# A delta-rule attention layer and two mixing blocks on one core: the first 32-row inversion alone on VectorE in two interleaved sets, v and k in one load, shorter and later weight conversions, and other durations in the planner

## The chip, the core and the metric

One NeuronCore of a Trainium2 chip runs the whole program. The metric is device time of one execution in microseconds (us). Engines: TensorE (PE; its weight loads are PEld), VectorE (DVE), ScalarE (ACT), GpSimd (POOL) and SyncE (SP), which issues all DMAs. The granted clock of TensorE is shown as a share of 2.4 GHz: 1.00 is 2.4 GHz, 0.50 is 1.2 GHz.

## The reference, cut to what matters

```python
k_n = k / (np.linalg.norm(k, axis=-1, keepdims=True) + 1e-06)      # q, k, v: [4, 8, 768, 48]
for t in range(S):                                                  # delta rule, one state 48x48 per head
    y[:, :, t] = einsum('bhd,bhde->bhe', q[:, :, t], state)
    v_old = einsum('bhde,bhd->bhe', state, k_n[:, :, t])
    state = state + beta_t * einsum('bhd,bhe->bhde', k_n[:, :, t], v[:, :, t] - v_old)
x = y as [4, 768, 384]
h = relu(x @ w_in); u, v = halves of h                              # first mixing block, w_in 384x1024
gated = u * (w_spatial @ layernorm(v) + b_spatial); x = gated @ w_out
theta = x @ w_theta                                                 # second mixing block
u = x + w_tok_r @ (x * cos(theta)) + w_tok_i @ (x * sin(theta))
out = u + relu(u @ w_ch)
```

The weights come in as float64 (as pairs of 32-bit words); activations are float32.

## The kernel before, in words

**Attention.** The sequence is cut into chunks of 64 tokens: 12 per batch, 48 in all, each with all 8 heads side by side. In a chunk the delta rule is a linear system with a unit triangular 64x64 matrix per head. Eight chunks make a round (six rounds). `norms(r)` computes the key norms of a round; `gram(g)` makes the products of keys on TensorE (line 551), which VectorE masks and scales into `GX` (line 556; the scaled mask `gm`, line 529, is made by GpSimd, in the first round also by VectorE); `invert(r)` inverts all 32 matrices of the round at once. It copies the diagonal 32x32 blocks together (`GX<-GX`), transposes them into `un` (line 574), does 30 elimination steps of two dependent instructions each (a product, line 585, and a sum, line 590), transposes back (lines 596 and 599), and finishes the 64x64 inverse with small matmuls (`mg`, lines 615 and 621). Rounds 2 and 4 do the 60 elimination instructions on GpSimd, the others on VectorE.

`chain(g)` is serial over chunks: `ru` of the state (line 685), the right-hand side `rt` (line 689; line 678 for the first chunk of a batch), `ru` of the inverse (line 696), the copies into `W`, and the state update `s` (line 712). `py` (line 724) is the chunk's output. `jit(g)` prepares what only chunk g needs; in it v and k are loaded apart and scaled apart (lines 661 and 657).

**Mixing blocks.** All their matmuls are issued by one line, 838, in three products of split float32 (fp32r) parts; they are called big matmuls here. The first block's weights are converted from float64 (`cvt` and `vl`, 12 pieces of 256 columns) before its first big matmul. The second block's weights (`bgt` and `bgm`, 68 pieces of 192 columns) are converted beside the first block and parked in DRAM tiles until it ends. A conversion is one ScalarE instruction (the absolute value of the high word) and four on VectorE (lines 747, 752, 756 and 759).

**Order.** Nothing is issued in program order. Every piece of work is a task with durations for the engines that may do it, dependences and a priority; the class `Plan` replays engines of these durations on the host and issues the tasks in the order in which they would start. An engine takes its instructions strictly in that order. All DMAs go through SP's queue in that order, too.

## Time and profile before

| | |
|---|---|
| median of 3 runs | 847.38 us (845.59, 847.38, 847.4) |
| profiled execution, span from first to last instruction | 849.1 us |
| busy: PE, DVE, ACT, POOL | 750.6, 638.9, 330.8, 253.1 us |
| mean granted clock of TensorE | 0.906 |
| instructions on DVE, POOL | 1503, 346 |

The profile gives the profiled execution's span; no time of its own stands beside it. The span is 1.7 us above the median of the runs, so a time worked out from the span is read as a run's time with 1.7 us taken off. Busy shares are averages over stages with different limits, so the stages are read apart below.

### The profile page before, as it was taken

How to read it: one execution, taken by the hardware profiler on the slowest of the kernel's cores; microseconds unless marked ns; L12 is line 12 of the kernel's file. 1: busy time of each engine (PE TensorE's matmuls, PEld its weight loads, DVE VectorE, ACT ScalarE, POOL GpSimd, SP SyncE). 2: the span in 40 equal slices, each digit the busy share in tenths (PEclk: the TensorE clock that was granted, in tenths of full speed). 3: DMA queues.
4: the chain of work that ended last, by engine and by line, in shares of the span. 5: the costliest groups of instructions: out<-in, count | busy, mean ns of one | idle time of the engine just before them, and what ended most of it. 6: DMA issues, size and time to landing. Idle time of an engine off the chain costs nothing. (4 is left out here: it accounts for less than half of the span.)

```text
span 849.1 us, 21902 instructions
## 1 busy us (share of the span) xinstructions
PE 750.6 (88%) x8672; PEld 689.2 (81%) x8672; DVE 638.9 (75%) x1503; ACT 330.8 (39%) x747; POOL 253.1 (30%) x346
## 2 busy tenths in 40 slices
PE   4317799899898897999998999979999999999998
PEld 4216677678886786888777999969999999999997
DVE  6899998997989779599876666387575565658544
ACT  4326237434244543243654334145332332333331
POOL 2442633476523358633221010032211111111010
PEclk8555589888899889999998999989999999999999
DMA  8826356676367666645666570234011101001001
GB/s 237 231 64 164 93 166 170 166 196 170 89 171 211 175 173 189 192 120 167 187 180 165 161 225 1 74 119 137 26 44 63 26 25 56 25 25 63 19 2 56
DMA packets 101701, 102.42 MB, mean 121 GB/s; under 512 B 10848, under 2 KB 86624, under 8 KB 101600
## 3 DMA queue, kind: packets, MB, share of 16 engines
q1 hardware_dynamic: 101600, 101.03, 41.5%
q8 instruction: 68, 1.11, 0.6%
q14 instruction: 33, 0.27, 0.1%
HBM read 74.38 MB, written 22.41 MB: 114 GB/s over the span
## 5 line engine op out<-in xcount | busy, mean ns | idle before, releaser
L838 PE MATMUL m<-w,vh 128*128 128x256 f32 x576 | 116.0, 301 | 1.0 <-ACT uT L364 1.0
L838 PEld LDWEIGHTS m<-w,vh 128*128 128x128 f32 x576 | 93.8, 201 | 4.5 <-ACT uT L364 1.2
L838 PE MATMUL y<-wr,z 128*128 128x384 f32 x432 | 87.9, 341 | 0.0
L838 PE MATMUL y<-w,z 128*128 128x384 f32 x432 | 85.0, 340 | 0.0
L838 PE MATMUL m<-w,vl 128*128 128x256 f32 x288 | 83.8, 291 | 0.0
L838 PEld LDWEIGHTS y<-wr,z 128*128 128x128 f32 x432 | 77.0, 190 | 0.0
L838 PEld LDWEIGHTS y<-w,z 128*128 128x128 f32 x432 | 75.5, 188 | 0.0
L838 PEld LDWEIGHTS m<-w,vl 128*128 128x128 f32 x288 | 57.6, 200 | 0.0
L696 PEld LDWEIGHTS ru<-rt,GX 64*64 64x64 f32 x384 | 30.4, 155 | 25.2 <-DVE rt L689 17.9
L696 PE MATMUL ru<-rt,GX 64*64 64x48 f32 x384 | 36.7, 243 | 15.7 <-DVE rt L689 14.4
L657 POOL TENSOR_TENSOR kc<-kc,gam 128x192 f32<-128x192 f32 x36 | 22.4, 623 | 93.1 <-DMA kc<-in_kn_dram 73.9
L838 PE MATMUL m<-wo,gh 128*128 128x384 f32 x192 | 48.8, 335 | 1.1 <-DVE rr L1145 1.1
L364 ACT ACTIVATE W<-ru 64x192 f32<-64x192 f32 x88 | 28.6, 326 | 53.8 <-PE ru L697 52.0
L615 PE MATMUL mg<-xt,GX 32*32 32x32 f32 x768 | 18.8, 203 | 34.6 <-DVE xt L596 27.8
L1143 DVE TENSOR_SCALAR ni<-m 128x384 int32<-128x384 f32 x24 | 13.3, 555 | 47.8 <-PE m L838 47.8
L529 POOL TENSOR_TENSOR gm<-mask,gam 128x256 f32<-128x256 f32 x59 | 39.5, 671 | 29.3 <-DVE pp L560 10.8
L615 PEld LDWEIGHTS mg<-xt,GX 32*32 32x32 f32 x768 | 16.0, 118 | 38.8 <-DVE xt L596 28.9
L585 DVE TENSOR_TENSOR tmp<-un 128x30 f32<-128x30 f32 (+14 forms) x120 | 46.4, 387 | 1.2
L838 PE MATMUL m<-xTh,wih 128*128 128x256 f32 x144 | 47.1, 327 | 0.0
L590 DVE TENSOR_TENSOR un<-un,tmp 128x30 f32<-128x30 f32 (+14 forms) x120 | 45.9, 383 | 1.2
L770 POOL TENSOR_TENSOR gl<-graw,gh 128x512 fp32r<-128x512 f32 x11 | 14.8, 1342 | 96.7 <-DVE gh L370 80.3
L364 ACT ACTIVATE bgm<-bgr 128x192 f32<-128x192 f32 x68 | 25.3, 375 | 45.2 <-DMA wdr<-bgm 12.1
(191 smaller groups left out, 2285.2 us busy)
## 6 DMA issues: line engine op xcount, KB each, us to landing
kq<-in_kqT_dram SPq DMA_DIRECT2D x96, 128.0 KB, 3.6
kg<-in_kqT_dram SPq DMA_DIRECT2D x32, 256.0 KB, 3.2
gd<-gt SPq DMA_DIRECT2D x24, 256.0 KB, 2.8
graw<-gd SPq DMA_DIRECT2D x24, 256.0 KB, 2.8
k<-in_kn_dram SPq DMA_DIRECT2D x24, 192.0 KB, 3.8
v<-in_vn_dram SPq DMA_DIRECT2D x48, 96.0 KB, 2.5
kc<-in_kn_dram SPq DMA_DIRECT2D x48, 96.0 KB, 3.1
xd<-xs SPq DMA_DIRECT2D x48, 96.0 KB, 2.7
```

The costliest lines, as they stand in the source:

```text
L364: nc.scalar.activation(out=out, in_=in_, func=func, **kw)
L529: eng[e].tensor_tensor(out=gm.t, in0=mask.t.unsqueeze(1).to_broadcast([128, HP, CH]), in1=gam[r].t[:, j].unsqueeze(2).to_broadcast([128, H ...
L585: eng[e].tensor_tensor(out=t3, in0=un.t[:, k:k + 1, 0:k].to_broadcast([128, m, k]), in1=un.t[:, k + 1:32, k:k + 1].to_broadcast([128, m, k ...
L590: eng[e].tensor_tensor(out=un.t[:, k + 1:32, 0:k], in0=un.t[:, k + 1:32, 0:k], in1=t3, op=ALU.add)
L615: mm(out=ps.t[q + 32:q + 64, u, :], lhsT=gx[q:q + 32, u0 + u, 32:64], rhs=xt.t[q:q + 32, u0 + u, :], start=True, stop=True, tile_position= ...
L657: lambda e: eng[e].tensor_tensor(out=kc.t, in0=kc.t, in1=gam[r].t[:, j].unsqueeze(2).to_broadcast([128, HP, D]), op=ALU.mult),
L696: mm(out=pu.t[64:128, hp, :], lhsT=gx[64:128, u, :], rhs=rt.t[64:128, hp, :], start=True, stop=True)
L770: P.add(o_tts(n), lambda e: eng[e].tensor_tensor(out=lv(), in0=mv(), in1=hv().bitcast(F32), op=ALU.subtract), [m, h], [(l, part)], pr)
L838: mm(out=view(), lhsT=a, rhs=c, start=(start and q == 0 and s_ == 0), stop=(stop and q == tot - 1 and s_ == 2))
L1143: P.add(o_dve(DM), lambda e: nc.vector.tensor_scalar(out=ni.t, in0=th(), scalar1=1.0 / TWO_PI, scalar2=None, op0=ALU.mult), [ps], [ni], pr)
```

## The change

1. **The first inversion.** In round 0 each elimination step is split over the even and the odd columns (`sets`), each with a scratch tile of its own: product even, product odd, sum even, sum odd. It makes 118 instructions of half the size out of 60. A list `inv0` holds the task that ends this inversion (the transpose back into `GX`); other VectorE work waits for it by `after=inv0`: the norms' reduction and the masks of later rounds, the first block's weight conversions and splits, the products in `jit`. The other rounds keep their 60 instructions.
2. **Loads.** v and k of a chunk lie beside each other in DRAM and come in one DMA of 192 KB into `vk`; one instruction of 384 columns scales both (for the first three chunks ScalarE does it in 24 small instructions). The norms read k by fours, not by twos. `G1P` puts the Gram products of round 1 at a later priority.
3. **Conversions.** The scratch `t` is gone. The absolute value is raised to a smallest number, masked and shifted in place: two instructions with one input and two with two inputs, where one with one input and three with two inputs stood. The second block's pieces are 384 columns wide (34 instead of 68 of each instruction), and they may start only when chunk 16's `ru` of the inverse has been issued (`BG0`).
4. **The planner.** Its durations are replaced (for instance a group of 8 matmuls 490 ns for 648), and it now models the time a semaphore takes from each engine to each other, a lock between VectorE and GpSimd for work that is not from PSUM, bytes and landings of DMAs, and a change of matmul kind on PE. So the order changes everywhere.

```diff
-KN = 4
+KN = 2
+KB = 4
-G1P = -19.8
-BGW = 192
+G1P = -9.5
+BGW = 384
+BG0 = 16
+ACTV = 3
...
-    SAME = {"PE": 0.0, "ACT": 60.0, "DVE": 127.0, "POOL": 90.0, "SP": 0.0, "X": 0.0}
-    CROSS = 190.0
+    SAME = {"PE": 0.0, "ACT": 142.0, "DVE": 126.0, "POOL": 133.0, "SP": 0.0, "X": 0.0}
+    TAIL = {"PE": 185.0, "ACT": 112.0, "DVE": 90.0, "POOL": 55.0, "SP": 0.0, "X": 0.0}
+    LAT = {"PE": 54.0, "ACT": 35.0, "DVE": 35.0, "POOL": 78.0, "SP": 27.0, "X": 0.0}
...
+                    if e == "SP":
+                        s = max(s, lands[-LANES])
+                    if e in self.HELD and held[e] != t.part:
+                        s = max(s, free[e] + self.HELD[e])
+                    if t.port and e in lock:
+                        b0, b1 = lock["POOL" if e == "DVE" else "DVE"]
+                        if b0 <= s < b1:
+                            s = b1
...
-        v_b[g] = r_v.new()
-        load(v_b[g], lambda: v_b[g].t, vn[b, c], 98304, pr)
-        kc_b[g] = r_kc.new()
-        load(kc_b[g], lambda: kc_b[g].t, kn[b, c], 98304, pr)
+        vk = vk_b[g] = r_vk.new()
+        load(vk, lambda: vk.t, vkn[b, c], 196608, pr)
...
+        sets = [(0, 1)] if not cr else [(0, 2), (1, 2)]
+        ub = [Buf(tile_=un.t) for _ in sets]
+        fin = [[] for _ in sets]
+        heads = []
         for k in range(30, 0, -1):
-            m = 31 - k
-            tmp = r_tmp.new()
...
+            for half in (0, 1):
+                for i, (c0, st) in enumerate(sets):
+                    t0 = k + 1 + (k + 1 - c0) % st
+                    m = len(range(t0, 32, st))
+                    if m <= 0:
+                        continue
+                    if half == 0:
+                        tmp = fin[i] = r_tmp.new()
...
+                                                 in1=un.t[:, t0:32:st, k:k + 1].to_broadcast([128, m, k]), op=ALU.mult)
...
+                            eng[e].tensor_tensor(out=un.t[:, t0:32:st, 0:k], in0=un.t[:, t0:32:st, 0:k], in1=t3, op=ALU.add)
...
+        if cr:
+            inv0.append(P.tasks[-1])
...
+        vk = vk_b[g]
+        if g < ACTV:
+            for i in range(2):
+                def fv(e, i=i):
+                    for hp in range(HP):
+                        act(vk.t[:, i, hp], vk.t[:, i, hp], ACTF.Copy, scale=ng_b[r].t[:, j, i, hp:hp + 1])
+
+                A([("ACT", 4 * 235.0)], fv, [ng_b[r]], [vk], pr)
+            return
+        A([("DVE", d_dve(384)), ("POOL", 880.0)],
+          lambda e: eng[e].tensor_tensor(out=vk.t, in0=vk.t, in1=ng_b[r].t[:, j].unsqueeze(3).to_broadcast([128, 2, HP, D]),
+                                         op=ALU.mult), [ng_b[r]], [vk], pr, after=inv0)
...
+        P.add([("DVE", d_dve2(n))], lambda e: nc.vector.tensor_scalar(
+            out=m.t, in0=m.t, scalar1=TINY_LO, scalar2=None, op0=ALU.max), [], [m], pr, after=inv0)
+        P.add([("DVE", d_dve2(n))], lambda e: nc.vector.tensor_scalar(
+            out=mi(), in0=mi(), scalar1=0x07FFFFFF, scalar2=3, op0=ALU.bitwise_and, op1=ALU.logical_shift_left), [], [m], pr)
+        P.add(o_dve(n), lambda e: nc.vector.scalar_tensor_tensor(
+            out=mi(), in0=lo(), scalar=29, in1=mi(), op0=ALU.logical_shift_right, op1=ALU.bitwise_or), [raw], [m], pr)
+        P.add(o_dve(n), lambda e: nc.vector.scalar_tensor_tensor(
+            out=mi(), in0=hi(), scalar=-0x40000000, in1=mi(), op0=ALU.bitwise_and, op1=ALU.bitwise_or), [raw], [m], pr)
```

What the new plan does to the order shows at two places on VectorE. The first is the beginning of round 0's inversion. `GX_108` is round 0's matrix and `GX_109` round 1's; `gm` is a scaled mask, `cvt` the scratch of a weight conversion, `un` and `tmp` belong to the inversion. Before:

```order
L513 SCALAR_TENSOR_TENSOR gam<-gam,beta_sb 128x32
L747 TENSOR_SCALAR cvt<-vh 128x256
L529 TENSOR_TENSOR gm<-mask,gam 128x256
L556 TENSOR_TENSOR GX_109<-gp,gm 128x256 x2
L529 TENSOR_TENSOR gm<-mask,gam 128x256
L574 STREAM_TRANSPOSE un<-GX_108 128x1024
L575 MEMSET un 128x32
L556 TENSOR_TENSOR GX_109<-gp,gm 128x256
L585 TENSOR_TENSOR tmp<-un 128x30
L590 TENSOR_TENSOR un<-un,tmp 128x30
L585 TENSOR_TENSOR tmp<-un 128x58
L556 TENSOR_TENSOR GX_109<-gp,gm 128x256
```

And now:

```order
L592 TENSOR_TENSOR GX_108<-gp,gm 128x256 x3
L407 COPY GX_108<-GX_108 32x32x32
L611 STREAM_TRANSPOSE un<-GX_108 128x1024
L612 MEMSET un 128x32
L633 TENSOR_TENSOR tmp<-un 128x30
L633 TENSOR_TENSOR tmp<-un 128x29
L641 TENSOR_TENSOR un<-un,tmp 128x30
L633 TENSOR_TENSOR tmp<-un 128x29
L641 TENSOR_TENSOR un<-un,tmp 128x29 x2
```

The work on round 1's norms and matrix and on the weights no longer stands ahead of or between the elimination steps. The six `GX_109` products that stood between them, and the two ahead of them, come behind the inversion.

The second place is the end of the same inversion, with the first chunk's right-hand side `rt`. Before, these rows led up to it, behind the transposes back and one copy; `ss` and `k` belong to later norms, `vl`, `vh` and `wil_138` to the weights:

```order
L747 TENSOR_SCALAR cvt<-vh 128x256
L499 TENSOR_REDUCE ss<-k 128x8
L770 TENSOR_TENSOR wil_138<-vl,wih_135 128x256
L752 SCALAR_TENSOR_TENSOR cvt<-vh,cvt 128x256
L499 TENSOR_REDUCE ss<-k 128x8
L756 SCALAR_TENSOR_TENSOR cvt<-vh,cvt 128x256
L759 SCALAR_TENSOR_TENSOR vl<-vl,cvt 128x256
L503 TENSOR_SCALAR ss<-ss 128x32
L678 TENSOR_SCALAR rt<-v 128x192
```

And now:

```order
L641 TENSOR_TENSOR un<-un,tmp 128x15 x2
L734 TENSOR_SCALAR rt<-vk 128x192
L646 STREAM_TRANSPOSE xt_620<-un 128x32x32
L649 STREAM_TRANSPOSE GX_108<-un 128x32x32
L407 COPY GX_108<-GX_108 32x32x32
L802 TENSOR_SCALAR vl<-vl 128x256 x2
L804 TENSOR_SCALAR vl<-vl 128x256 x2
L806 SCALAR_TENSOR_TENSOR vl<-vh,vl 128x256 x2
L808 SCALAR_TENSOR_TENSOR vl<-vh,vl 128x256 x2
```

The right-hand side now stands straight behind the last elimination step; the conversions of the first block's weights, two pieces of which stood ahead of `rt` before, all stand behind the inversion.

## Rows read from the trace of the kernel before

**Rows 1.** Stretches: us, then busy us (instructions) by engine; PEclk, DMA share, GB/s.

```profile
21.00:58.00 37.00, 8.53 (x142) 7.08 (x140) 33.19 (x71) 10.54 (x21) 13.09 (x18) 0.50 0.56 159
66.00:138.85 72.85, 59.38 (x1062) 50.00 (x1062) 71.50 (x196) 35.40 (x92) 32.27 (x39) 0.69 0.50 140
138.85:234.95 96.10, 85.44 (x1235) 74.01 (x1228) 85.04 (x201) 37.91 (x89) 57.11 (x94) 0.86 0.58 162
234.95:372.10 137.15, 123.33 (x2096) 105.64 (x2090) 112.80 (x289) 57.81 (x142) 66.13 (x106) 0.93 0.64 176
372.10:482.00 109.90, 103.23 (x1707) 88.09 (x1700) 84.09 (x245) 53.11 (x136) 23.80 (x30) 0.95 0.61 171
482.00:849.10 367.10, 358.04 (x2206) 352.36 (x2202) 230.14 (x445) 122.50 (x249) 49.75 (x41) 0.99 0.19 60
```

**Rows 2.** Stretches, line 696 alone (8 instructions a chunk): PE, PEld, PEclk, DMA.

```profile
66.00:138.85 72.85, 7.38 (x64) 6.24 (x64) 0.69 0.50 140
138.85:234.95 96.10, 6.56 (x64) 5.46 (x64) 0.86 0.58 162
234.95:372.10 137.15, 11.35 (x128) 9.33 (x128) 0.93 0.64 176
```

**Rows 3.** Timeline ahead of the first inversion: start, us, instruction, [idle before, releaser].

```profile
15.20 0.74 DVE L556 TENSOR_TENSOR GX<-gp,gm 128x256 f32<-128x256 f32 x2
16.46 0.42 DVE L556 TENSOR_TENSOR GX<-gp,gm 128x256 f32<-128x256 f32 x1 [0.52 <-PE gp L551]
18.42 0.43 ACT L364 ACTIVATE vl<-vh 128x256 f32<-128x256 f32 x1 [2.82 <-DMA vh<-in_w_in_dram]
18.86 2.12 ACT L364 ACTIVATE GX<-GX 32x1024 f32<-32x1024 f32 x2
21.02 1.95 DVE L574 STREAM_TRANSPOSE un<-GX 128x1024 f32<-128x1024 f32 x1 [0.57 <-ACT GX L364]
```

**Rows 4.** Timeline of VectorE and GpSimd in the first inversion.

```profile
23.34 0.18 DVE L585 TENSOR_TENSOR tmp<-un 128x30 f32<-128x30 f32 x1
...
43.98 1.07 DVE L590 TENSOR_TENSOR un<-un,tmp 128x228 f32<-128x228 f32 x1
45.08 0.39 DVE L585 TENSOR_TENSOR tmp<-un 128x220 f32<-128x220 f32 x1
...
53.86 0.21 DVE L590 TENSOR_TENSOR un<-un,tmp 128x30 f32<-128x30 f32 x1
...
42.69 2.10 POOL L770 TENSOR_TENSOR w<-gt,w 128x384 fp32r<-128x384 f32 x2 [1.89 <-ACT w L364]
```

**Rows 5.** Timeline of VectorE behind the first inversion.

```profile
57.89 0.68 DVE L370 COPY GX<-GX 32x1024 f32<-32x1024 f32 x1
...
65.70 0.25 DVE L678 TENSOR_SCALAR rt<-v 128x192 f32<-128x192 f32 x1
```

**Rows 6.** Groups by line and form on VectorE: count, busy us, mean ns, idle before.

```profile
L752 DVE SCALAR_TENSOR_TENSOR bgt<-bgr,bgt 128x192 int32<-128x192 int32 x68 | 29.9, 440 | 1.0
L756 DVE SCALAR_TENSOR_TENSOR bgt<-bgr,bgt 128x192 int32<-128x192 int32 x68 | 29.4, 432 | 1.1
L759 DVE SCALAR_TENSOR_TENSOR bgm<-bgm,bgt 128x192 f32<-128x192 f32 x68 | 27.7, 407 | 4.2 <-ACT bgm L364 2.4
L747 DVE TENSOR_SCALAR bgt<-bgr 128x192 int32<-128x192 int32 x68 | 23.6, 347 | 9.2 <-DMA bgr<-in_w_i_dram 3.9 <-DMA bgr<-in_w_r_dram 1.9 <-DMA bgr<-in_w_out_dram 1.2
L1147 DVE SCALAR_TENSOR_TENSOR rr<-ni,rr 128x384 f32<-128x384 int32 x24 | 14.4, 598 | 0.7
L1150 DVE TENSOR_SCALAR rr<-rr 128x384 f32<-128x384 f32 x24 | 8.6, 357 | 0.7
```

**Rows 7.** Timeline of GpSimd: first and last step of round 2's inversion.

```profile
166.68 0.23 POOL L585 TENSOR_TENSOR tmp<-un 128x30 f32<-128x30 f32 x1 [1.00 <-DVE un L574]
...
222.57 0.26 POOL L590 TENSOR_TENSOR un<-un,tmp 128x30 f32<-128x30 f32 x1
```

**Rows 8.** The chain that ended last: start, us, what.

```profile
511.21 31.55 PE m L838 x231
```

More of the change, by code (lines that the diff above doesn't have):

```diff
@@ L109, with add @@
 class Task:
-    __slots__ = ("opts", "fn", "deps", "prio", "extra", "crit", "users", "left", "eng", "start", "end", "allocs", "uid", "big", "act", "credit", "order", "banks")
+    __slots__ = ("opts", "fn", "deps", "prio", "extra", "crit", "users", "left", "eng", "start", "end", "allocs", "uid", "big", "act", "credit", "order", "banks", "port", "part", "mode")
 class Plan:
     ENGS = ("PE", "ACT", "DVE", "POOL", "SP", "X")
-    SAME = {"PE": 0.0, "ACT": 60.0, "DVE": 127.0, "POOL": 90.0, "SP": 0.0, "X": 0.0}
-    CROSS = 190.0
+    SAME = {"PE": 0.0, "ACT": 142.0, "DVE": 126.0, "POOL": 133.0, "SP": 0.0, "X": 0.0}
+    TAIL = {"PE": 185.0, "ACT": 112.0, "DVE": 90.0, "POOL": 55.0, "SP": 0.0, "X": 0.0}
+    LAT = {"PE": 54.0, "ACT": 35.0, "DVE": 35.0, "POOL": 78.0, "SP": 27.0, "X": 0.0}
+    HELD = {"ACT": 138.0, "DVE": 107.0}
     def __init__(self):
         self.tasks = []
-    def add(self, opts, fn, reads=(), writes=(), prio=0.0, extra=0.0, crit=False, after=(), big=False, act=0.292):
+    def add(self, opts, fn, reads=(), writes=(), prio=0.0, extra=0.0, crit=False, after=(), big=False, act=0.292,
+            port=True, part=0, mode=1):
         t = Task()
+        t.port, t.part, t.mode = port, part, 0 if big else mode
         t.big, t.act, t.credit = big, 0.98 if big else act, 0.0
@@ L226, in run @@
         free = dict.fromkeys(self.ENGS, 0.0)
+        held = dict.fromkeys(self.ENGS, 0)
+        lock = {"DVE": (0.0, 0.0), "POOL": (0.0, 0.0)}
+        mode = 0
+        lands, dmaq = [0.0] * LANES, 0.0
         cand = [t for t in self.tasks if t.left == 0]
@@ L243, in run @@
                     for d in deps:
-                        x = d.end + d.extra + (self.SAME[e] if d.eng == e else self.CROSS)
+                        x = d.end + d.extra + (self.SAME[e] if d.eng == e else self.TAIL[d.eng] + self.LAT[e])
                         if x > r:
@@ L271, in run @@
             if e == "PE":
-                if t.big and not self.pbig:
-                    t.start = s = s + 67.0
-                self.pbig = t.big
+                if t.mode != mode:
+                    t.start = s = s + (100.0 if mode else 140.0)
+                mode = t.mode
                 t.end = self.pe_run(t, s, dur)[0]
@@ L278, in run @@
                     self.credit -= dur
+            if e == "SP":
+                dmaq = max(dmaq, t.end + DMA_PRE) + dur.n / DMA_BW
+                t.extra = dmaq + DMA_POST - t.end
+                lands.append(dmaq + DMA_POST)
             free[e] = t.end
+            held[e] = t.part
+            if t.port and e in lock:
+                lock[e] = (s, t.end - (45.0 if e == "POOL" else 0.0))
             for b in t.banks:
@@ L529, in f @@
             eng[e].tensor_tensor(out=gm.t, in0=mask.t.unsqueeze(1).to_broadcast([128, HP, CH]),
-                                 in1=gam[r].t[:, j].unsqueeze(2).to_broadcast([128, HP, CH]), op=ALU.mult)
-        A([("POOL", 575.0)] + (o_dve(256) if pr < -10 else []), f, [gam[r], mask], [gm], pr, crit=pr < -10).order.add(mt)
+                                 in1=ng_b[r].t[:, j, 1].unsqueeze(2).to_broadcast([128, HP, CH]), op=ALU.mult)
+        A([("POOL", 575.0)] + (o_dve(256) if pr < -10 else []), f, [ng_b[r], mask], [gm], pr, crit=pr < -10, after=inv0).order.add(mt)
         return gm
@@ L601, in invert @@
+        A([("DVE", 1900.0)], lambda e: nc.vector.transpose(out=gx[:, :, 0:32].rearrange("p u t -> p t u"), in_=un.t),
+          [un] + ub, gg, pr + 0.1, crit=cr, port=False)
+        if cr:
+            inv0.append(P.tasks[-1])
         for q in (1, 3):
             A(o_cps(1024), lambda e, q=q: copy(e, gx[32 * q:32 * q + 32, :, 32:64], gx[32 * q:32 * q + 32, :, 0:32]),
-              [], [gg[q]], pr + 0.2, crit=cr)
+              [], [gg[q]], pr + 0.2, crit=cr, part=32 * q)
         for q in (1, 3):
@@ L648, in jit @@
                                                                             in1=gm.t[p0:p0 + 64], op=ALU.mult),
-                  [ps, gm], [(kq, True)], pr)
+                  [ps, gm], [(kq, True)], pr, port=False, part=p0, after=inv0)
         else:
@@ L770, in split @@
         P.add(o_tts(n), lambda e: eng[e].tensor_tensor(out=lv(), in0=mv(), in1=hv().bitcast(F32), op=ALU.subtract),
-              [m, h], [(l, part)], pr)
+              [m, h], [(l, part)], pr, after=inv0)
     r_wsp = ring("w3", "w3", [128, S], F32R, 2 * NT)
```

237 lines of the change are left out of this document (109 added, 128 removed).

## The prediction

> **What bounds the kernel now.** I read the busy times by stretch first, then the starts of the chunks, then the timeline where the first stretch is lost.
>
> From 482 us to the end TensorE is busy 358.0 of 367.1 us at a clock of 0.99 [rows 1]: all chunks are done, and only big matmuls are left. Nothing in the change touches their number, so this tail can only lose what has been done earlier. It bounds the end: whatever brings the last chunk forward brings the end forward.
>
> The chain of chunks runs from 66 to 482 us. Line 696 has 8 instructions a chunk, so the counts say where chunks begin [rows 2]: chunk 8 at 138.85 us, chunk 16 at 234.95, chunk 32 at 372.1. In the stretch to chunk 8 VectorE is busy 71.5 of 72.85 us: it is the bound there, and every microsecond added or taken counts. To chunk 16 it is busy 85.0 of 96.1 us, but there GpSimd inverts round 2, from 166.7 to 222.8 us [rows 7], and chunk 16 needs that; its 0.23 and 0.26 us first and last steps stand 56 us apart. From chunk 16 to 32 TensorE (123.3 of 137.15 us) and VectorE (112.8) are both nearly full, and from 372 us TensorE is (103.2 of 109.9) while VectorE has 26 us to spare [rows 1].
>
> Before 66 us there is no chain. In the 37 us from 21 to 58 us TensorE does 8.5 us of work and VectorE 33.2 [rows 1]: the first inversion is on VectorE and nothing else can go on. This is where the change acts first.
>
> **The start.** Round 0's last `GX` ends at 16.88 us; ScalarE's copies follow only at 18.86 us, because ahead of them stands a weight's `vl` that waits for its DMA until 18.42, and the transpose starts at 21.02 [rows 3]. Now one copy goes to VectorE (0.68 us, the row of [rows 5]) beside ScalarE's single one (half of 2.12 us), and the weights' loads stand ahead of eight other loads. The norms wait for a larger load now, which I put at 0.8 us. I take the transpose at 18.0 us, 3 us earlier; bounds 17.5 and 20.5.
>
> The 60 steps run from 23.34 to 54.07 us, 30.7 us [rows 4]. A step starts 0.03 us after the one before ends (43.98 + 1.07 to 45.08), so one of 30 elements, which lasts 0.21 us, costs 0.24 and one of 220 elements 0.42: about 0.2 us and 1/960 us an element. The smallest of the first steps are a little quicker (0.18), so I use 0.19 + n/960. Both halves of all steps have 9,920 elements, 10.3 us; 60 x 0.19 + 10.3 = 21.7 us clean. The other 9 us are round 1's six products between the steps and steps that take 1.07 us where their neighbour takes 0.39, under a GpSimd product from SBUF (42.69 to 44.79) [rows 4]. `inv0` keeps both away.
>
> The 118 half steps: each needs the result of two steps back, not of the last one. Two products of 256 elements without a dependence take 0.74 us together, where one takes 0.42 [rows 3]: a second one costs 0.32, or 0.055 + n/960. The planner's order puts an independent instruction between any dependent pair, and I take 0.066 us a step (some pairs are small): 118 x 0.066 + 10.3 = 18.1 us. If nothing overlaps, it is 118 x 0.19 + 10.3 = 32.7 us. The row for independent products is the nearest, so I take 18.1.
>
> The skill speaks against this edit: the Trainium skill, VectorE: DVE Perf Modes, section The DRAIN you can't avoid, says that the next VectorE instruction waits for the pipe of the last one to empty, with or without a semaphore, and its rules for authors ask for fewer instructions. The pair of 0.74 us disagrees, but it reads PSUM. By that rule the steps take the 32.7 us of the paragraph above and the start gains 14.6 us less, and this is a rival below.
>
> So the steps end at 18.0 + 2.1 + 0.2 + 18.1 = 38.4 us, where before it was 54.07. From the last step to chunk 0's line 696 it was 12.0 us: 4.5 us until the copy's end at 58.57, and then 7.1 us in which `rt` stood behind conversions and reductions until 65.70 [rows 5]. `rt` is now ahead of the transposes. Left are the transposes (3.8), the longer of the two copies (1.06), and, as I put them, 2 us of GpSimd's clearing, for which the matrices now wait, and 1.6 us of `mg` and its copy: about 8.5 us. Chunk 0 at 47 us instead of 66: **-19 us** (bounds: -4.5 without overlap, -21).
>
> **What comes back behind it.** Work on round 1 that stood ahead of the inversion or in it is done after it now: the 4.1 us that VectorE had from 16.88 to 21.02 [rows 3], six `GX_109` products at 0.42, and four reductions of 384 elements, which at the 0.42 us of 256 are 2.5 us: about 9 us. Two weight conversions more come to 3.3 us at the price below. VectorE has no room there (71.5 of 72.85 us). Against it stand the three pieces of second-block weights that were done before chunk 8 and now start behind chunk 16: a piece of 192 columns costs 0.440 + 0.432 + 0.407 + 0.347 = 1.63 us [rows 6], 4.9 us together. 9 + 3.3 - 4.9 is **+7 us** (bounds 12 if the second-block pieces were done in gaps, 4 if steps of 1 us fall away as above); chunk 8 at about 127 us.
>
> **The conversions.** 384 columns cost 2 x 1.63 = 3.25 us. The new form has two instructions with one input, for which the nearest row is 0.357 us at 384 columns, and two with two inputs, 0.598 [rows 6]: 1.91 us. That is 1.34 us less for each of 34, 46 us of VectorE in all. But it is worth something only where VectorE is waited for. By the order of instructions, 13 old pieces (21 us) stood before chunk 16's right-hand side, and none does now; 28 (46 us) stood between chunks 16 and 32, and now 15 of the new (29 us). To chunk 16 the inversion on GpSimd sets the pace: it begins once round 2's Gram products are done, near chunk 11, and those come sooner with a freer VectorE; it shares GpSimd with 11 other instructions instead of 14. I take **-5 us** of the 21 (bounds 0 and -12). Between chunks 16 and 32 the relief is 17 us, but the order also has 408 big matmuls there where 330 were: 78 at 31.55/231 = 0.137 us [rows 8] are 10.7 us of a TensorE with 14 us to spare. I take **0** (bounds -12 and +10). From 32 on VectorE had room; **0** (bounds 5 either way).
>
> **v and k together.** 48 loads fewer, and one instruction of 384 columns for two of 192. At a chunk every 9 us and three buffers, the scaling is needed two chunks after the load: its cover is 18 us against under 2 us of landing and scaling more. Without that cover it would cost up to 1 us a chunk. The first three chunks' 24 small ScalarE instructions lie beside the 18 us of steps, with ScalarE busy 10.5 of 37 us there [rows 1]; priced at the 0.43 us of 256 columns [rows 3] or less, they take at most 10 us. Both cost nothing.
>
> **The tail.** In the order 990 big matmuls stood before chunk 47's line 696, now 1,074. These 84 no longer lie behind it: 84 x 0.137 = 11.5 us, less as they are mostly of the shorter kind; **-10 us**. The rest of the tail is as full as before and unchanged.
>
> **Sum.** -19 + 7 - 5 + 0 + 0 - 10 = -27: a span of 849.1 - 27 = 822.1 us, and with the 1.7 us by which the span stands above the median **820 us**.
>
> **Rivals.**
> - *The half steps don't overlap.* 14.6 us of the start go: 820 + 14.6 = 835 us. For it: the steps of the trace all wait for their predecessor, so no row shows an overlap of two from SBUF alone. Against: the pair of 0.74.
> - *TensorE binds the chain.* It was busy 371 of 416 us; with 84 big matmuls more and the full debt, the start is given back: -19 + 12 + 0 + 10 - 10 = -7, 840 us. For it: the 123.3 of 137.15. Against: at 0.69 and 0.86 of the clock up to chunk 16 a busy TensorE is not a full one.
> - *The clock falls (slower).* The granted clock from 66 to 482 us averages 0.88, at 1.2 GHz in parts. If the new order of small and big matmuls leaves it lower, the busy 371 us stretch in proportion: the 27 us are lost at 0.82, and at 0.80 they are +37, 857 us. For it: nothing but the sensitivity; the first big matmuls come between chunks 3 and 4 in both orders. Against: the order has as many big matmuls ahead of each chunk or more.
> - *VectorE's relief counts in full.* -19 + 4 - 12 - 12 - 2 - 10 = -51, 796 us, if GpSimd's inversions start as early as VectorE lets them.
>
> **Chances.** Forecast (806 to 831) 0.58; no overlap 0.12; TensorE binds 0.13; the clock 0.08; full relief 0.09. Within 0.3% of 847.4 (2.5 us, about what a measurement of this kernel can tell from no change) fall parts of the second and third rivals: 0.03. Slower is the rest of the clock's: 0.08. Faster 0.89. The range is 800 to 845 us: it leaves out the clock and half of the full relief, 0.13.
>
> **What would show it.** Chunk 0's line 696 near 47 us, chunk 8 near 127, chunk 16 near 215, the last chunk near 465. The steps of round 0 from about 20 to 38 us, with starts 0.07 us + n/960 apart; if they lie 0.19 + n/960 apart, the first rival is right. No step of 1 us there. VectorE's busy time down by some 50 us. It is wrong if chunk 8 comes no earlier than 135 us, if chunk 16 waits for GpSimd as late as before, or if the stretch from 66 us shows a clock well under 0.88.

## The result and the profile after

The changed kernel takes 822.0 us (median of 4 runs, 819.97 to 824.94), the kernel before 846.49 us beside it; the ratio is 0.972 (95% interval 0.9687 to 0.9753). The forecast was 820 us in a range of 800 to 845. The profiled execution has a span of 821.2 us. The total came out within 2 us, but two of its terms were wrong by 12 and 6 us, in opposite directions, so much of that agreement is luck.

Busy times of the page; TensorE and VectorE have 13.9 and 40.2 us less than before:

```profile
PE 736.7 (90%) x8672; PEld 677.4 (82%) x8672; DVE 598.7 (73%) x1377; ACT 341.2 (42%) x757; POOL 222.8 (27%) x299
```

The stretches between the same chunks as in [rows 1] (the clock's records begin at 67.8 us in this execution, and what lies before is counted as 1.00: the 1.00 of the first row is no granted clock, and the 0.79 of the second is too high; from 67.8 us to chunk 8 it is 0.72, where before it was 0.69):

```profile
17.00:38.00 21.00, 3.12 (x32) 2.42 (x32) 20.89 (x122) 8.08 (x30) 0.00 (x0) 1.00 0.64 193
45.50:137.30 91.80, 68.33 (x1196) 58.66 (x1192) 83.95 (x222) 44.03 (x99) 40.12 (x48) 0.79 0.49 142
137.30:222.60 85.30, 81.31 (x1254) 72.01 (x1252) 52.92 (x112) 29.83 (x67) 51.95 (x87) 0.93 0.42 118
222.60:355.30 132.70, 125.47 (x2178) 107.28 (x2170) 117.82 (x269) 66.62 (x153) 62.55 (x92) 1.00 0.74 215
355.30:461.20 105.90, 98.87 (x1684) 84.06 (x1680) 86.27 (x209) 53.74 (x131) 19.05 (x18) 0.98 0.70 202
461.20:821.20 360.00, 348.58 (x2127) 342.99 (x2126) 219.72 (x417) 128.37 (x262) 39.65 (x36) 0.99 0.18 58
```

The `ru` of the inverse (line 752 now, 8 instructions a chunk; the 65th of the first row is chunk 8's first), as in [rows 2]:

```profile
45.40:137.30 91.90, 7.41 (x65) 6.27 (x65) 0.79 0.49 142
137.30:222.60 85.30, 5.67 (x64) 4.65 (x64) 0.93 0.42 118
222.60:355.20 132.60, 10.58 (x128) 8.60 (x128) 1.00 0.74 215
```

Chunk 0 begins at 45.5 us (66.1 before), chunk 8 at 137.3 (138.9), chunk 16 at 222.6 (235.0), chunk 32 at 355.3 (372.2), chunk 47 at 461.2 (481.7). So 20.6 us are won at chunk 0, 1.6 are left at chunk 8, and 27.9 are there at the end.

VectorE's timeline at the first inversion, against [rows 3] to [rows 5], and at the transposing of round 1:

```profile
15.46 0.68 DVE L407 COPY GX<-GX 32x1024 f32<-32x1024 f32 x1
16.55 1.95 DVE L611 STREAM_TRANSPOSE un<-GX 128x1024 f32<-128x1024 f32 x1 [0.40 <-ACT GX L401]
18.57 0.15 DVE L633 TENSOR_TENSOR tmp<-un 128x30 f32<-128x30 f32 x1
...
30.21 0.48 DVE L633 TENSOR_TENSOR tmp<-un 128x108 f32<-128x108 f32 x2
30.58 0.48 DVE L641 TENSOR_TENSOR un<-un,tmp 128x108 f32<-128x108 f32 x2
30.96 0.48 DVE L633 TENSOR_TENSOR tmp<-un 128x110 f32<-128x110 f32 x2
...
37.39 0.25 DVE L734 TENSOR_SCALAR rt<-vk 128x192 f32<-128x192 f32 x1
...
78.06 1.93 DVE L611 STREAM_TRANSPOSE un<-GX 128x1024 f32<-128x1024 f32 x1
```

The 118 half steps take 18.9 us where the 60 took 30.7. Four of 108 elements start in 0.75 us, 0.19 us apart, though a pair of them lasts 0.48. None takes 1 us, and GpSimd does nothing beside them (0.00 in the first row of the stretches).

What VectorE does from the end of this inversion to the transposing of round 1, 42 to 78 us (the six costliest groups: count, busy us, mean ns, idle before):

```profile
L534 DVE TENSOR_REDUCE ss<-k 128x16 f32<-128x768 f32 x6 | 5.5, 945 | 1.2 <-ACT k L401 1.1
L802 DVE TENSOR_SCALAR vl<-vl 128x256 f32<-128x256 f32 x10 | 4.8, 495 | 0.0
L806 DVE SCALAR_TENSOR_TENSOR vl<-vh,vl 128x256 int32<-128x256 int32 x8 | 4.5, 566 | 0.0
L815 DVE TENSOR_TENSOR wil<-vl,wih 128x256 fp32r<-128x256 f32 x7 | 4.0, 571 | 0.0
L804 DVE TENSOR_SCALAR vl<-vl 128x256 int32<-128x256 int32 x9 | 3.8, 429 | 0.0
L808 DVE SCALAR_TENSOR_TENSOR vl<-vh,vl 128x256 int32<-128x256 int32 x8 | 3.3, 428 | 0.0
```

The five rows of first-block weights (all but the first) add up to 20.4 us of these 36, or to 17.8 when each instruction is counted only until the next one starts; 8 of the 12 pieces are finished before round 1 is transposed, where before the change there were 3. Round 1's transposing now comes 4.2 us later than before (it was at 73.82 us).

GpSimd's inversion of round 2, first and last step, against [rows 7]: 45.3 us instead of 56.1.

```profile
164.22 0.24 POOL L633 TENSOR_TENSOR tmp<-un 128x30 f32<-128x30 f32 x1
...
209.21 0.27 POOL L641 TENSOR_TENSOR un<-un,tmp 128x30 f32<-128x30 f32 x1
```

Its 60 steps take 32.8 us of these (33.4 before); 11 other instructions stand between them (14), 7.1 us (9.8); and GpSimd is idle 6.1 us there instead of 13.8 (neighbours overlap a little, so the three add up to a bit more than the whole).

The second block's conversions, against [rows 6]:

```profile
L808 DVE SCALAR_TENSOR_TENSOR bgm<-bgr,bgm 128x384 int32<-128x384 int32 x34 | 21.1, 620 | 0.3
L806 DVE SCALAR_TENSOR_TENSOR bgm<-bgr,bgm 128x384 int32<-128x384 int32 x34 | 20.6, 608 | 0.3
L802 DVE TENSOR_SCALAR bgm<-bgm 128x384 f32<-128x384 f32 x34 | 16.0, 474 | 9.3 <-ACT bgm L401 9.2
L804 DVE TENSOR_SCALAR bgm<-bgm 128x384 int32<-128x384 int32 x34 | 14.5, 430 | 0.3
```

A piece costs 2.13 us in the mean (1.82 by the median durations 359, 355, 554 and 555 ns; some are stretched to 1 us and more), 1.12 less than 3.25. By medians it is 0.84 less: two of the old half-size pieces are 2.66 us (259, 358, 357 and 358 ns an instruction).

One sum that the prediction did not make: a span is TensorE's busy time and its idle time. Before, these were 750.6 and 98.5 us; now 736.7 and 84.5. Half of the gain is TensorE waiting less, half is the same 8672 matmuls taking less time. From 67.8 us on, where both executions have a record, TensorE's clock is at 0.50 for 62.5 us; before, it was for 111.1.

### The profile page after: what moved, and what is told of

Read it like the earlier page. It is cut to its first block, busy times and chain, and to the rows that moved or that the text cites. A ratio compares the mean times of both kernels' runs of the same rounds, so it can differ in the third digit from the quotient of the medians.

```text
span 821.2 us, 21423 instructions
## 1 busy us (share of the span) xinstructions
PE 736.7 (90%) x8672; PEld 677.4 (82%) x8672; DVE 598.7 (73%) x1377; ACT 341.2 (42%) x757; POOL 222.8 (27%) x299
## 4 chain that ended last, share of the span: by engine, by line
PE 56%; DVE 26%; DMA 8%; issue 4%; ACT 2%; SPq 2%; POOL 2%; POOLq 0%; DVEq 0%; ACTq 0%
PE m L882 27%; PE y L882 19%; DVE tmp L633 4%; DVE un L641 4%; DMA vk<-in_vkn_dram 2%; PE gp L587 2%; DMA kq<-pp 2%; PE ru L752 1%; PE py L780 1%; DMA bgr<-in_w_r_dram 1%; DVE GX L649 1%; PE s L768 1%; DVE xt L646 1%; PE ru L741 1%; DMA k<-in_vkn_dram 1%
## 5 line engine op out<-in xcount | busy, mean ns | idle before, releaser
L882 PE MATMUL m<-w,vh 128*128 128x256 f32 x576 | 110.8, 291 | 1.7 <-DVE gt L990 1.2
L882 PEld LDWEIGHTS m<-w,vh 128*128 128x128 f32 x576 | 88.9, 190 | 5.4 <-DVE gt L990 1.3
L565 POOL TENSOR_TENSOR gm<-mask,ng 128x256 f32<-128x256 f32 x63 | 41.8, 670 | 75.8 <-DVE pp L596 52.3
L1188 DVE TENSOR_SCALAR ni<-m 128x384 int32<-128x384 f32 x24 | 13.3, 556 | 57.8 <-PE m L882 57.8
L633 DVE TENSOR_TENSOR tmp<-un 128x58 f32<-128x58 f32 (+23 forms) x149 | 49.1, 348 | 0.9
L752 PEld LDWEIGHTS ru<-rt,GX 64*64 64x64 f32 x384 | 28.3, 145 | 24.5 <-DVE rt L745 19.7
L641 DVE TENSOR_TENSOR un<-un,tmp 128x58 f32<-128x58 f32 (+23 forms) x149 | 44.5, 316 | 0.7
L401 ACT ACTIVATE x<-m 128x384 f32<-128x384 f32 x15 | 7.3, 489 | 87.0 <-PE m L882 87.0
L882 PE MATMUL m<-xTl,wih 128*128 128x256 f32 x144 | 41.0, 285 | 0.0
L882 PE MATMUL m<-xTh,wil 128*128 128x256 f32 x144 | 40.9, 284 | 0.0
L587 PE MATMUL gp<-kg 48*64 48x128 f32 x512 | 37.9, 289 | 3.1 <-DVE pp L596 1.8
L882 PE MATMUL m<-wt,xh 128*128 128x384 f32 x144 | 37.4, 341 | 2.8 <-ACT xh L401 2.8
```

The lines of the kernel that those rows point to most:

```text
L401: nc.scalar.activation(out=out, in_=in_, func=func, **kw)
L565: eng[e].tensor_tensor(out=gm.t, in0=mask.t.unsqueeze(1).to_broadcast([128, HP, CH]), in1=ng_b[r].t[:, j, 1].unsqueeze(2).to_broadcast([12 ...
L587: mm(out=pv()[o:o + 64, hp, :], lhsT=kh, rhs=kg.t[i:i + D, :, hp, :] if fused else kh, start=True, stop=True)
L633: eng[e].tensor_tensor(out=t3, in0=un.t[:, k:k + 1, 0:k].to_broadcast([128, m, k]), in1=un.t[:, t0:32:st, k:k + 1].to_broadcast([128, m, k ...
L641: eng[e].tensor_tensor(out=un.t[:, t0:32:st, 0:k], in0=un.t[:, t0:32:st, 0:k], in1=t3, op=ALU.add)
L752: mm(out=pu.t[64:128, hp, :], lhsT=gx[64:128, u, :], rhs=rt.t[64:128, hp, :], start=True, stop=True)
```

## The experiments

All are edits of the changed kernel. Most edits lead the planner to a new order of everything; where the order was kept, the text says so. Differences are against 822.0 us, and the ratio is to the kernel before on the same chip. The kernel before took 843.4, 844.6 and 843.6 us beside these runs and 846.5 beside the changed kernel, which did not run again with them; so a difference of 3 us or less is not to be read, and small ones are given by the ratios, too.

**Dependent half steps.** One task issues a set's product and sum together:

```diff
-                        heads.append(A([(en, dur)], fa, ...))
...
-                        A([(en, dur)], fb, ...).order.update(heads[-3:])
+                A([(en, 4 * d_dve((31 - k) * k / 2))], fp, [], [un] + tms, ...)   # fp: product, sum of even; product, sum of odd
```

> The 118 half steps of round 0 stay, but in the order product even, sum even, product odd, sum odd, so that about 74 of them need the result of the step just ahead (59 sums, and every second product of an even set) and 44 do not. Everything else that VectorE does stands behind them as in the changed kernel. Theory A (the steps of the changed kernel overlap because neighbours are independent): dependent steps cost 0.19 us + n/960, independent ones 0.066 us + n/960, so the inversion's steps take 74 x 0.19 + 44 x 0.066 + 10.3 = 27.3 us where the changed kernel took 18.9. Theory B (a half step is cheap whatever stands ahead of it): 19 us. Theory C (no two steps ever overlap, and something else made the 18.9): 118 x 0.19 + 10.3 = 32.7 us. The second question is what the first inversion's time is worth at the end: if all VectorE work up to chunk 8 is queued behind it (theory P, it passes through), chunk 0, the transposing of round 1 and chunk 8 all come some 8 us later and the kernel takes 828 us (825 to 831). If it is given back on the way (theory Q), chunk 0 comes 8 us later, chunk 8 less than 3 us later, and the kernel takes 822 to 824 us.

845.24 us (1.0011, 0.9979 to 1.0044). The steps took 26.1 us (18.6 to 44.7): theory A. Chunk 0 came 7.1 us later and chunk 8 5.5, but chunk 32 17.6, and behind the last chunk 2,118 big matmuls were left instead of 2,022. Further on the new order was another one, so the 23 us do not answer the second question. The next run does: the product is issued straight ahead of its sum, and the planner isn't told.

```diff
-                        heads.append(A([(en, dur)], fa, ...))
+                        late[i] = fa
+                        heads.append(A([(en, dur)], lambda e: None, ...))
...
+                            late[i](e)      # in fb: the product is issued straight ahead of its sum
```

> The same dependent order of the half steps as in e1_dependent_steps (each product straight ahead of its sum), but the planner isn't told: every other instruction of every engine stands where it stands in the changed kernel. So the first 7 us or so of e1_dependent_steps come without its new order from chunk 8 on. Theory P (a microsecond in VectorE's queue ahead of chunk 8 is a microsecond at the end, as 7.4 us at chunk 8 were 10.1 at the end without the first weights): steps of 26 us, chunk 0 near 52.6, chunk 8 at 143 to 145, 828 to 831 us. Theory R (the queues, made for earlier times, lose much more behind it): 835 us or more. Theory Q (it is given back by chunk 16 or later): 821 to 824 us.

827.48 us (0.9821, 0.9769 to 0.9872): half a microsecond below theory P's range, 5.5 us more than the changed kernel (8.5 by the ratios). Its VectorE timeline:

```profile
34.11 0.26 DVE L633 TENSOR_TENSOR tmp<-un 128x108 f32<-128x108 f32 x1
34.41 0.27 DVE L645 TENSOR_TENSOR un<-un,tmp 128x108 f32<-128x108 f32 x1
34.60 0.28 DVE L633 TENSOR_TENSOR tmp<-un 128x120 f32<-128x120 f32 x1
34.91 0.28 DVE L645 TENSOR_TENSOR un<-un,tmp 128x120 f32<-128x120 f32 x1
```

A sum starts 0.30 us after the product that it needs; the next product, which does not need that sum, starts 0.19 us after it. The first is 0.19 + 108/960, the second close to 0.066 + 108/960 = 0.18: both of the prediction's prices, in one row of instructions. Five of the six executions took 826.0 to 831.5 us, and the profiled one, the only one with a trace, 838.1; in it TensorE ran at half its clock for 24 us while it was fully busy:

```profile
417.10:440.90 23.80, 23.80 (x333) 21.53 (x334) 12.73 (x36) 11.04 (x27) 2.02 (x2) 0.50 0.47 138
```

**No hold.** `inv0` stays empty:

```diff
-        if cr:
-            inv0.append(P.tasks[-1])
```

> The list inv0 stays empty: no VectorE work is held back until round 0's inversion ends; everything else is as changed, in a new plan. Theory P (only the sequence of a full VectorE changes): the steps stretch from 18.9 us to 26 to 32 us and chunk 0 comes at 52 to 58 us instead of 45.5, but the work on round 1 and on the first weights is done earlier by as much, so round 1's transposing stays within 3 us of the changed kernel's 78.1 us, chunk 8 within 4 us of 137.3 us and the whole within 820 to 826 us. Theory H (keeping the inversion alone is where the gain is, since work between the steps also breaks their pairs and brings GpSimd's products beside them): chunk 8 at 143 us or later and 830 us or more.

825.86 us (0.9811, 0.9778 to 0.9844), 3.9 us more than the changed kernel (7.7 by the ratios). The total is theory P's; the way is neither's. The steps took 21.3 us, chunk 0 came at 54.7 us, round 1's transposing at 89.9 (not within 3 us of 78.1) and chunk 8 at 146.1, but chunk 16 at 209.7, 13 us earlier than in the changed kernel.

**First weights left out.** VectorE's four instructions of each first-block piece are not issued; the order is kept:

```diff
+        skip = n < 384
-        P.add([("DVE", d_dve2(n))], lambda e: nc.vector.tensor_scalar(
+        P.add([("DVE", d_dve2(n))], lambda e: None if skip else nc.vector.tensor_scalar(      # and the three behind it
```

> VectorE leaves out the four instructions of each of the 12 conversions of the first block's weights (48 instructions, 16.8 us at 0.28, 0.28, 0.41 and 0.41 us, more where they were stretched); the planner believes that they are there, so the order of everything else is that of the changed kernel. The weights of the first block are then not converted. Theory D (the loss behind the start is VectorE's work: round 1's transposing and its 43 us of steps stand in one queue with the conversions, and chunk 8 waits for that inversion): round 1's transposing comes at 66 to 72 us instead of 78.1, its last step at 106 to 114 instead of 124.2, chunk 8 at 121 to 128 us instead of 137.3; the kernel ends 4 to 12 us earlier, 810 to 818 us, since GpSimd's inversion of round 2 and TensorE take over later. Theory E (chunk 8 is held by TensorE at half its clock, or by the chain of chunks itself): chunk 8 moves by less than 4 us and the whole by less than 2 us.

812.93 us (0.9648, 0.9617 to 0.9679): theory D, with less than its numbers ahead of chunk 8. Round 1's transposing:

```profile
71.09 1.95 DVE L611 STREAM_TRANSPOSE un<-GX 128x1024 f32<-128x1024 f32 x1 [0.29 <-ACT GX L401]
```

7.0 us earlier; the last step at 116.4 us, chunk 8 at 129.9 (7.4 earlier), chunk 16 7.9, chunk 32 8.9, chunk 47 9.8, the end 10.1 earlier (9.1 by the medians of the runs, 6.1 by the ratios). VectorE's busy time fell by 14.6 us in all, so not every microsecond taken out of its queue comes through: from 41.4 us to this transposing VectorE is idle for 7.5 us, where it was for 2.9 in the changed kernel. What does come through to the transposing is there at chunk 8 and, roughly, at the end.

**Chain first.** The first four chunks get priority:

```diff
-        pr = float(g)
+        pr = g - 30.0 if g < 4 else float(g)
```

> The tasks of the chain of chunks 0 to 3 get priorities ahead of round 1's and the weights' work (g - 30 for g), so that the right-hand sides of chunks 1, 2 and 3 no longer stand behind them in VectorE's queue; in the order 11 rows of chunk 1's way and some 40 of chunk 2's go behind. Theory D (chunk 8 waits for round 1's inversion, and chunks 1 to 7 have time): chunk 2 comes at 64 to 72 us instead of 80.5, but round 1's transposing stays at 77 to 81 us, chunk 8 at 134 to 140 us, and the whole at 819 to 825 us. Theory F (the loss is the place of the right-hand sides of chunks 1 and 2, which come 5 and 11 us after their operands are there): chunk 8 comes 8 to 12 us earlier, near 127 us, and the whole 5 to 10 us, 812 to 817 us.

839.15 us (0.9952, 0.9922 to 0.9982), outside both. VectorE's rows of chunks 1 to 3 and round 1:

```profile
54.70 0.36 DVE L745 TENSOR_TENSOR rt<-ru,vk 128x192 f32<-128x192 f32 x1
62.58 0.36 DVE L745 TENSOR_TENSOR rt<-ru,vk 128x192 f32<-128x192 f32 x1 [0.79 <-PE ru L742]
69.42 0.35 DVE L745 TENSOR_TENSOR rt<-ru,vk 128x192 f32<-128x192 f32 x1
82.42 2.01 DVE L611 STREAM_TRANSPOSE un<-GX 128x1024 f32<-128x1024 f32 x1
```

Chunk 2 came 17 us earlier, at 63.5 us. Round 1's transposing came 4.4 us later, and chunk 8 7.6 us later, at 144.9. So theory F is refuted, as far as an order of its own can show it: it is not the place of the right-hand sides that holds chunk 8.

**The old price of the conversions**, the order kept:

```diff
-            out=m.t, in0=m.t, scalar1=TINY_LO, scalar2=None, op0=ALU.max)
+            out=m.t, in0=m.t, scalar=TINY_LO, in1=m.t, op0=ALU.max, op1=ALU.max)        # n == 384
...
+            for _ in range(2 if n == 384 else 1):       # f3, f4: each or-instruction twice
```

> The 34 conversions of the second block's weights take VectorE about as long as the old form did: the smallest-number instruction has two inputs, and the two instructions that combine the halves are issued twice (their result is the same), so a piece costs 2 x 0.555 + 2 x 0.555 + 0.555 + 0.355 = 3.1 us instead of 1.82, 44 us more in all between 228 and 462 us. The order of all other instructions is that of the changed kernel. Theory V (VectorE is waited for from chunk 16 to 47, so the shorter form is a gain of its own): the last chunk 12 to 40 us later and 834 to 860 us. Theory T (TensorE and the inversions set the pace there, VectorE has room): the last chunk less than 5 us later, 821 to 827 us.

857.22 us (1.0127, 1.0077 to 1.0176): theory V. Chunks 16 to 32 and 32 to 47 in the profiled execution, the longest of the six (863.2 us):

```profile
224.90:382.30 157.40, 141.05 (x2176) 120.48 (x2168) 141.34 (x302) 66.59 (x153) 67.91 (x92) 0.88 0.62 182
382.30:501.30 119.00, 103.04 (x1690) 87.52 (x1682) 107.50 (x242) 53.55 (x131) 19.09 (x18) 0.94 0.62 180
```

24.7 and 13.1 us more than in the changed kernel. VectorE is busy 90% of both; TensorE waits 32.3 us instead of 14.3, and its clock falls from 1.00 and 0.98 to 0.88 and 0.94, with 244.1 us busy instead of 224.3. So about half of the 37.8 us are waits and half the lower clock. The edit is also dearer than the old form: it adds 44 us to VectorE by the medians (47 us of busy time), where 34 pieces at the old price would add 29 (38 by the means). In proportion, the shorter form is worth 23 to 28 us, an estimate from these numbers. With the planner told of the price:

```diff
-        P.add([("DVE", d_dve2(n))], (...max...)
+        P.add([("DVE", d_dve(n) if n == 384 else d_dve2(n))], (...max...)
-        P.add(o_dve(n), f3, ...)
+        P.add([("DVE", (2 if n == 384 else 1) * d_dve(n))], f3, ...)        # and f4
```

> The longer conversions of f2_old_price_order_kept again, 44 us of VectorE more, but now the planner is told (the two doubled instructions and the one with two inputs have their durations), so it makes an order of its own. Theory V (the work itself is waited for): 840 to 860 us, the last chunk at 475 us or later. Theory B (in f2 the queues were blind to the longer pieces, and a plan that knows them puts them where VectorE has room): 820 to 832 us. Between the two lies what the shorter form is worth when the order may follow it. A plan's luck of some 17 us, as in the control, is in this number.

853.85 us (1.0119, 1.0063 to 1.0175), the last chunk at 484.4 us: theory V again, and by more than a plan's luck of 17 us; from chunk 16 to 47 TensorE waits 31.6 us here, too. It is the work that is waited for, not only an order blind to it.

**Round 1's products early.** `G1P` as it was before the change:

```diff
-G1P = -9.5
+G1P = -19.8
```

> G1P is set back to -19.8, so the Gram products and the matrix of round 1 take priority over the weights' conversions behind the first inversion; a new plan. Theory D (chunk 8 waits for round 1's inversion, which waits for its matrix in VectorE's queue): round 1's transposing 2 to 5 us earlier than 78.1 us and chunk 8 at 132 to 136 us, the whole 812 to 820 us. Theory W (the weights are only put behind and come back in the steps): transposing earlier, steps longer, chunk 8 within 2 us of 137.3 and the whole 818 to 826 us.

817.81 us (0.9706, 0.9661 to 0.9752). Round 1's transposing stayed (78.0 us) and its steps took longer (until 131.6), so of theory W only the longer steps hold, and of theory D only the total; chunk 8 came at 141.1, outside both. The interval overlaps that of the changed kernel, so this part of the change shows no gain.

**A control.** One planner number is moved by 5 ns, the work is the same:

```diff
-    TAIL = {"PE": 185.0, ...
+    TAIL = {"PE": 190.0, ...
```

> A control: one number of the planner, the time that a semaphore from TensorE takes, is 190 ns instead of 185 ns. No instruction is added, removed or changed; only the order that the planner works out. If the order that comes out of a plan is worth the same whatever small thing was changed (theory N), the kernel takes 819 to 825 us. If a plan's later stages are a matter of luck (theory L), the start is the same (chunk 0 at 45 to 46 us), the stages behind chunk 16 differ by 5 to 20 us, and the whole lies outside 817 to 827 us.

839.06 us (0.9931, 0.9897 to 0.9965): theory L, 17 us for nothing. Its last chunk came at 457.7 us, 3.5 earlier than in the changed kernel, but 2,190 big matmuls were left behind it. Where it lost, a stretch of the control, and then the like stretch of the changed kernel:

```profile
395.00:442.70 47.70, 42.55 (x666) 37.23 (x668) 32.88 (x78) 24.68 (x59) 4.99 (x5) 0.50 0.77 224
```

```profile
398.00:446.00 48.00, 44.54 (x824) 38.21 (x825) 34.95 (x78) 26.54 (x67) 8.46 (x7) 1.00 0.76 217
```

Both are about as busy; at half the clock 666 matmuls were done, at the full one 824.

**The old model of waits** in the planner:

```diff
+    SAME = {"PE": 0.0, "ACT": 60.0, "DVE": 127.0, "POOL": 90.0, "SP": 0.0, "X": 0.0}
+    TAIL = dict.fromkeys(ENGS, 190.0)
+    LAT = dict.fromkeys(ENGS, 0.0)
+    HELD = {}
...
+        lock = {}
...
-                dmaq = max(dmaq, t.end + DMA_PRE) + dur.n / DMA_BW
```

> The changed kernel with the old model of waits in the planner: one time between engines (190 ns), the old times within an engine, no lock between VectorE and GpSimd, no cost for a change of matmul kind but the old 67 ns, a DMA that lands a fixed 2200 ns after its issue. The durations of the instructions stay new. Theory M (the measured waits are a part of the gain, since an order made for other waits puts instructions ahead of ones that are ready): 832 to 850 us. Theory O (any order will do within luck): 815 to 831 us.

835.28 us (0.99, 0.9851 to 0.9949): theory M, but by 13 us, less than the control. Its chunk 47 came at 436.2 us, 25 us earlier than in the changed kernel, and still it ended later. The big matmuls (its line 875) behind the last chunk, and then those of the changed kernel (line 882):

```profile
436.20:830.20 394.00, 375.29 (x2236) 361.39 (x2235) 0.99 0.20 64
```

```profile
461.20:821.20 360.00, 345.07 (x2023) 333.82 (x2022) 0.99 0.18 58
```

213 more were left for later, and they took 30 us of TensorE.

**Other orders of the same work.** Only priorities and limits are set anew (one line for all of them here):

```diff
# h1
-XP, BURST, TPR, GPR, NPR, G1P, BG0 = 1092.5, 6000, 3, 4, -1.5, -9.5, 16
+XP, BURST, TPR, GPR, NPR, G1P, BG0 = 1095, 8000, 2, 5, 1, -19.8, 17
# h2
-XP, WP0, GPR, IPR, NPR = 1092.5, -19.0, 4, 0, -1.5
+XP, WP0, GPR, IPR, NPR = 1100, -5.0, 5, 1, -4
```

> Seven priorities and limits of the planner are set anew (G1P, NPR, GPR, TPR, XP, BURST, BG0); the work is the same instruction by instruction. Theory L (the order is worth as much as the parts of the change): 798 to 812 us, chunk 8 at 130 to 136 us, the last chunk at 430 to 445 us and no more than 30 us of the span behind 140 us at half the clock. Theory F (near 818 us TensorE's work and the start leave nothing to win): 816 to 826 us.

> Another five of them (NPR, GPR, IPR, XP, WP0), with the first weights' conversions behind round 1's products; the same work. Theory L: 798 to 815 us, chunk 1 some 8 us later than 60 us but chunk 8 at 128 to 136 us. Theory F: 816 to 826 us.

809.77 us (0.9596, 0.9556 to 0.9636) and 804.17 us (0.9524, 0.9487 to 0.956): theory L both times, with chunk 8 later than it said (139.1 and 138.0 us). The second is the fastest version of this study, 17.8 us under the changed kernel. Its stretches from chunk 0, 8, 16, 32 and 47 on (its clock is recorded from 106.4 us only, so the 0.98 of the first row is no granted clock; from there to chunk 8 it is 0.95):

```profile
45.30:138.00 92.70, 76.70 (x1257) 65.50 (x1253) 90.18 (x230) 45.49 (x101) 45.10 (x54) 0.98 0.52 151
138.00:201.70 63.70, 61.28 (x1117) 53.42 (x1111) 47.54 (x107) 30.52 (x69) 46.64 (x78) 0.97 0.47 135
201.70:332.10 130.40, 124.83 (x2177) 108.25 (x2176) 119.88 (x273) 62.93 (x143) 64.04 (x92) 1.00 0.73 215
332.10:433.70 101.60, 95.44 (x1657) 80.66 (x1656) 82.93 (x216) 51.90 (x125) 12.91 (x13) 0.98 0.72 211
433.70:802.40 368.70, 359.56 (x2223) 353.49 (x2222) 223.65 (x425) 129.64 (x263) 37.07 (x33) 1.00 0.18 58
```

Against the changed kernel it has one stretch that is 21.6 us shorter, chunks 8 to 16, and a tail 8.7 us longer. TensorE is idle 70.6 us of its span (802.5 - 731.9).

## Why the forecast was right, and where it was not

| term | forecast, bounds | measured |
|---|---|---|
| start, chunk 0 | -19 (-4.5, -21) | -20.6 |
| debt, chunk 0 to 8 | +7 (+4, +12) | +19.0 |
| chunk 8 to 16 | -5 (0, -12) | -10.8 |
| chunk 16 to 32 | 0 (-12, +10) | -4.5 |
| chunk 32 to 47 | 0 (5 either way) | -3.6 |
| tail | -10 | -7.4 |
| sum | -27 | -27.9 |

The measured terms are those of the two profiled executions; by the medians of the runs the gain is 24.5 us. The misses (-1.6, +12.0, -5.8, -4.5, -3.6 and +2.6 us) cancel. Nothing in the prediction makes them cancel, and 5 ns in the planner move the total by 17 us: that the sum is met so closely is luck.

**The start was right by its steps.** Transposing at 16.55 us (18.0 forecast, 17.5 its lower bound), steps of 18.9 us (18.1), from the copy's rows to chunk 0 as worked out. The rival that half steps don't overlap, 32.7 us, is out: 18.9 us in the kernel, 25.9 when 59 pairs were made dependent at the same places, at the two prices of the prediction. The prediction named the Trainium skill, VectorE: DVE Perf Modes, section The DRAIN you can't avoid, on the side of this rival, but read only part of it: the section goes on that a next instruction that is not held starts earlier. The trace agrees with that sentence (0.19 us from start to start where each lasts 0.27 to 0.29), and not with a wait behind every instruction. With the order kept, 7 us of lost overlap were 5.5 us at the end (8.5 by the ratios).

**The debt is the step that failed**, outside its bounds; chunk 8 at 137.3 us is also past the 135 us that the prediction named as a sign of being wrong. It added up VectorE's work between chunk 0 and chunk 8 and held that VectorE has no room there. The work is 83.95 us now where it was 71.50, and VectorE is idle for 7.85 us where it was for 1.35: these 12.4 and 6.5 us are the 19. The terms that the prediction named came out near their sum. Counting each instruction until the next one starts, round 1's norms and matrices have 6.8 us more (9 forecast), the first block's weights 3.4 more (3.3) and the second block's 3.4 less (4.9). What it put at nothing is the rest: 5.5 us of other VectorE work (masking of `kq`, copies of `W`, scaling of `vk`, longer steps) and the idle time, 4.1 us of it in two waits between 131 and 137 us, when round 1's steps are done.

What it did not name either is what the weights stand ahead of: round 1's transposing, whose steps (80.7 to 124.2 us) chunk 8 waits for. 8 pieces instead of 3 are finished before it, and some of their instructions took 0.65 us where 0.28 is usual. From the end of round 0's inversion to that transposing it was 15 us before and is 36 now. That this queue holds chunk 8 was shown: without VectorE's part of all twelve pieces the transposing, chunk 8 and the end of the profiled execution came 7.0, 7.4 and 10.1 us earlier. That the chain's own places do not hold it is what the run with the chain first says. The pieces are at most 7.4 of the 19 us; the other parts were counted in the trace, and no run tried them one by one.

**Chunk 8 to 16 was right in its mechanism, as the trace has it, and too small in size.** GpSimd's inversion set the pace, with 11 instructions between its steps instead of 14, as counted from the order. The prediction gave this 5 us; it was 10.8. The inversion is 10.9 us shorter, 2.7 of it by the instructions and 7.7 by waits between the steps that are gone, which the prediction did not name. No run tried this stretch by itself.

**The zeros from chunk 16 to 47 hid the largest term.** The prediction let TensorE bind there and gave the cheaper conversions nothing. A dearer form than the old one cost 35 us with the order kept and 32 in an order of its own, in proportion 23 to 28 us for the old form: VectorE's work is waited for from chunk 16 to 47, though TensorE's busy time looks fuller. The measured stage shrank by only 8 us because the change also moves conversions into it: none of the 34 pieces is done by chunk 16 and 17 are between chunks 16 and 32, where before 20 of the 68 half-size ones were done by chunk 16 and 21 between. The sentence that VectorE had room from chunk 32 on is wrong (13.1 us more in that stage with the dearer form). VectorE's busy time fell by 40.2 us, not by the 46 to 50 of the prediction, since stretched instructions keep a piece at 2.13 us where 1.91 was forecast.

**The tail** was right in mechanism: 2,022 big matmuls behind the last chunk instead of 2,106, the 84 of the prediction. But its premise, that whatever brings the last chunk forward brings the end forward, fell. With the old model of waits that chunk came 25 us earlier and the end 9 us later (profiled executions). The end moves by TensorE's idle time and by its time at half the clock.

**The clock rival** did not come true here: the granted clock rose (1.00 from chunk 16 to 32, where it was 0.93). It did in the control (TensorE's busy time 754.8 us instead of 736.7 for the same matmuls) and in the profiled execution of the order-kept run. The prediction said that nothing but the sensitivity speaks for it; in these runs a chance order, or a chance execution, was enough.

**How much of the 25 us is the change, and how much the order that it happened to get?** The overlap (5.5 to 8.5 us) and the conversions' price (an estimated 23 to 28) are shown with the order kept. The hold (+3.9 us undone), `G1P` (-4.2 undone) and the planner's waits (+13.3 undone) are smaller than what 5 ns in one number do, so their own worth stays open. v and k in one load, the late start of the second block's weights and the planner's new durations were not tried alone. So the prediction's nothing for the loads is not shown; the chain that ended last spends 1.9% of the span, some 16 us, on loads of `vk`.

## What to carry to other kernels

Where one full engine feeds the next long serial piece (here VectorE and round 1's inversion), look for what a moved block now stands ahead of, not only for how much is moved. Make a second sum beside that of the serial chain: the idle time of the engine that does the bulk of the work, and its time at the lower clock, since a chain that ends sooner with less bulk work done can win nothing (here 25 us at the last chunk, and 9 us lost at the end). And where a planner orders everything, move one of its numbers by a trifle and time it first: a part is measured only by a run that keeps the order, or when it is worth more than that control.
